# Windowed attention and a hardswish MLP on one core: the output weights loaded before batch 1, and the order of the first 80 microseconds rewritten around that

## The chip, the core and the metric

The kernel runs on 1 core of one Trainium2 chip. The core has a matrix engine (TensorE, PE in the profile), a vector engine (VectorE, DVE), a scalar engine (ScalarE, ACT), GpSimd (POOL) and SyncE (SP), and 16 DMA engines that all queues share. Each engine works through its own list of instructions in order, so an instruction that waits holds up everything listed behind it. The metric is the device time of one execution in microseconds (us), and shorter is better.

## The reference

Attention with a causal window of 64 over 8 batches of 576 tokens, 8 heads of 64; its output, 4608 tokens of 512 values, goes through two matrix products with a hardswish between them.

```python
batch, n_heads, seq, head_dim = (8, 8, 576, 64)
n_tokens, d_model, d_ff = (4608, 512, 2048)
# attention
scores = scale * np.matmul(q, k.transpose(0, 1, 3, 2))
rel = pos[:, None] - pos[None, :]
mask = (rel >= 0) & (rel < window)            # window = 64
scores = np.where(mask, scores, -1000000000.0)
attn = np.exp(scores - max); attn = attn / (sum + 1e-09)
attn_out = np.matmul(attn, v)
# MLP, x = attn_out as (4608, 512)
h = x @ w_in
g = h * np.clip(h + 3.0, 0.0, 6.0) / 6.0
out = g @ w_out
```

The inputs are float32 in DRAM; the loads issued by POOL turn them into bfloat16 on the way into SBUF, and the output is float32.

## The kernel before

**Two kinds of work.** The attention is done two heads at a time: a step `t` is one pair of heads of one batch, four steps (`NG` = 4) to a batch, 32 in all. The MLP is done in blocks of 512 tokens (`TB`), nine in all. A batch has 576 tokens, so block 0 needs only batch 0, and block 1 needs the end of batch 0 and most of batch 1.

**The units of the MLP.** A *first unit* (`unit` in `first_units`, line 472) is four matmuls that make one tile `hT` of 128x512; then ACT makes `t` from it (line 480) and DVE makes one of the 16 columns of `gT` (line 481). Only when DVE is done is the PSUM buffer of `hT` free again. A *second unit* (`unit` in `second_units`, line 500) is four matmuls that add four of those columns, times `wout`, into a tile `acc`; four second units make 128 tokens, which ACT copies to `osb` (line 506) and SP stores (line 508). A block has 16 first units and 16 second units, the second ones as four times four. In this text f8 is the first unit of column 8 of a block, and s0 to s15 are its second units.

**The step of attention**, from batch 1 on: `turn` transposes q and k with matmuls into two PSUM tiles `tk` and `tq` (line 272), `turned` copies them to `KT` (DVE) and `QZ` (ACT) (line 279), `s_first` and `s_rest` make the scores (lines 292, 306), `weights` takes the exponent on ACT (lines 315, 318) and multiplies by a 0/1 band into `P` and `Pz` (lines 323, 326), on POOL or, where the caller says so, on DVE; `pv` multiplies by the values (line 393), `pv_out` divides on DVE (lines 402 to 412), and `x_` moves the result to `xT` by a DMA transpose on SP (line 426), or `x_turned` by matmuls and a copy on ACT (lines 441 to 447). `turn_two` is `turn` and both copies; `front` is the scores and the weights.

**The values** are kept twice, as they come (`Un`) and shifted by 64 tokens (`Us`). `load_v` loads `Un` and the last part of `Us` from DRAM; `shift` then makes the rest of `Us` from `Un` with two SBUF-to-SBUF DMAs on SP (lines 154, 155).

**PSUM.** `ps_t` has three buffers (scores, `hT`, the transposed output), `ps_h` two (`tk` and `tq`, `hT` at some places), `ps_o` one (the result of `pv`), `ps_acc` one (`acc`, and in the first block every second `hT`).

**The order** is written out by hand at the end of the kernel. MLP units wait in a queue, `moe`; `weave(n)` takes n of them. `queue_block(kb)` puts in the 16 first units of block kb, and between them the 16 second units of the block before, which were kept in `left`. Batch 0 has its own early path. Then come the steps of batch 1, with the first units of block 0 between them one at a time, then some units of block 1, and from `group(7, 2)` on a regular loop: `group(t, n)` does `pv(t)`, `turn(t + 2)`, the scores and weights of t + 1, and n units. `late[0]` chooses the PSUM pools.

**The loads.** POOL issues them in program order: q, k and v of batch 0, `w_in` in three parts (line 160), q and k of batch 1 for two steps, v of batch 1, the rest of q and k of batch 1, then `w_out` in two halves (line 166). Each of these DMAs waits until the one eight before it has landed.

The code that the change touches, with the line numbers that the profile uses:

Of the kernel before, what the change touches and what calls it, by code (L numbers as in the profile page):

```python
# [24 lines left out]
P = 128  # L25
D = 64
W = 64
# [9 lines left out]
def kernel(  # L37
# [9 lines left out]
    nc = tc.nc  # L47
# [66 lines left out]
    def load_qk(b, n=NG, first=0):  # L114
        t = staged[b] if first else stage.tile([P, H, RL * D], BF16, name="qk9", tag="qk")
        hs = slice(2 * first, 2 * (first + n))
        for z, src in enumerate((k, q)):
            nc.gpsimd.dma_start(
                out=t[halves[z], hs], in_=src[b, hs].rearrange("h (p r) d -> p h (r d)", r=RL)
            )  # L120
        return t
# [5 lines left out]
                out=Vn[0][:n, m, :, 0:D], in_=v[0, :, m * P : m * P + n, :].rearrange("h s d -> s h d"),  # L127
            )

    def load_v(b):  # L130
        for m in range(3):
            to = Un[b % 2][:, m] if m < 2 else Us[b % 2][3 * P // 4 : P, 1]
            n = 2 * to.shape[0]
            nc.gpsimd.dma_start(  # L134
                out=to[:, :, VO : VO + P],
                in_=v[b, :, 2 * P * m : 2 * P * m + n, :].rearrange("h (p r) d -> p h (r d)", r=2),
            )

    def pads(b, memset):
        for t in (Un[b % 2], Us[b % 2]):  # L140
            memset(t[:, :, :, 0:VO], 1.0)
            memset(t[:, :, :, VO + P : VW], 1.0)
# [345 lines left out]
    def second_units(kb):  # L488
        gT = gTs.pop(kb)
        units = []  # L490
        for ts in range(TB // P):
            state = {}

            def unit(i, ts=ts, state=state):
                if i == 0:
                    pool = ps_t if late[0] == 2 and ts % 2 else ps_acc
                    state["acc"] = pool.tile([P, DM], F32, name="acc", tag="bk")
                acc = state["acc"]
                for fc in range(4 * i, 4 * i + 4):
# [14 lines left out]

    left = []

    def queue_block(kb):

        f, n = first_units(kb), len(left)
        for i, unit in enumerate(f):  # L520
            moe.extend(left[i * n // NFC : (i + 1) * n // NFC])
            moe.append(unit)
        left[:] = second_units(kb)

    def queue_last(kb):

        queue_block(kb)
        queue_block(kb + 1)
        moe.extend(left)
        left.clear()  # L530

    def begin(kb, pools, between):

# [7 lines left out]
    def weave(n):  # L541
        for _ in range(min(n, len(moe))):
            moe.popleft()()
# [108 lines left out]
    for i in range(3):  # L652
        load_w_in(i)
    late_windows()
    staged[1] = load_qk(1, 2)
    load_v(1)
    shift(1)
    load_qk(1, 2, 2)
    for i in range(2):
        load_w_out(i)  # L660
    nc.vector.memset(recs[:], 1.0)
    zero_rows(1)
    nc.vector.memset(Pl[0][:], 1.0)
# [32 lines left out]
    x_early(1)  # L696
    pv_early(3)
    x_early(2)
    queue_block(0)
    begin(0, (ps_acc, ps_t, ps_t), lambda: x_early(3))  # L700
    def group(t, n):

# [21 lines left out]
    def turn_two(t):  # L724
        turn(t)
        turned(t, 0)
        turned(t, 1)

    def front(t, host, muls=(nc.gpsimd,) * 3):
        s = s_first(t, host)  # L730
        weights(t, s, s_rest(t), muls)

    both = (nc.gpsimd, nc.vector, nc.vector)
    n = NG
    weave(4)
    turn_two(n)
    weave(1)
    turn_two(n + 1)
    front(n, n + 1)
    weave(1)  # L740
    front(n + 1, n + 1, both)
    weave(1)
    pv(n)
    pv_out(n)
    x_(n)
    weave(1)
    turn_two(n + 2)
    pv(n + 1)
    pv_out(n + 1)
    x_(n + 1)  # L750
    weave(1)
    turn_two(n + 3)
    front(n + 2, n + 3, both)
    weave(1)
    front(n + 3, n + 3, both)
    weave(1)
    pads(2, nc.gpsimd.memset)
    staged[2] = load_qk(2)
    load_v(2)
    pv(n + 2)  # L760
    pv_out(n + 2)
    weave(1)
# [1 line left out]
    pv_out(n + 3)  # L764
    x_turned(n + 2)
    weave(len(moe))
    late[0] = 1
    queue_block(1)
    weave(1)
    x_turned(n + 3)  # L770
    shift(2)
    weave(9)
    turn_two(2 * NG)
    weave(2)
    group(2 * NG - 1, 2)
    staged[3] = load_qk(3)
    pads(3, nc.gpsimd.memset)
    load_v(3)
    for t in range(2 * NG, T):
# [48 lines left out]
```

## Time and profile before

| what | value |
|---|---|
| time, median of 3 runs | 336.35 us (334.4 to 337.25) |
| time of the profiled execution | 338.35 us |
| its span, first to last instruction | 336.6 us |
| mean granted TensorE clock | 0.974 of full speed |
| PE busy | 308.8 us (92%) |
| ACT, DVE, POOL busy | 188.8, 175.9, 120.4 us |
| moved by DMA | 36.03 MB, mean 107 GB/s |
| one `t` (ACT, line 480), one `gT` (DVE, line 481) | 687 ns, 687 ns |
| one `Pz` on POOL (line 326) | 1145 ns median |
| one `KT` copy (DVE), one `QZ` copy (ACT) | 740 ns, 633 ns |

In the profile, "busy" is the time in which an engine executes; the slices and windows tell where in the span it does. The chain of waits is followed back from the last instruction and tells what released each step. The granted clock is the share of full speed at which PE ran. The times of the runs and the profile's span differ by what lies around the span: 338.35 - 336.6 = 1.75 us for the profiled execution.

### The profile page before, as it was taken

To read this page: it belongs to the slowest core of one execution; us is meant where nothing else is said; L and a number is where in the kernel's file an instruction comes from. 1 tells how busy PE (TensorE), PEld (TensorE's weight loads), DVE (VectorE), ACT (ScalarE), POOL (GpSimd) and SP (SyncE) were. 2 spreads that over 40 slices of the span, in tenths; PEclk is the share of its full clock that TensorE was granted. 3 is DMA by queue.
4 is the path that set the end of the run, shared out by engine and by line. 5 is a ranking of instruction groups with operands and counts; after the bars stand their busy time and mean duration, and the time that the engine had idled before them with its cause. 6 is when DMAs were issued, how large, how long until landed. Compare 5 with 4: busy or idle time off the path is not lost.

```text
span 336.6 us, 11066 instructions
## 1 busy us (share of the span) xinstructions
PE 308.8 (92%) x4770; PEld 157.8 (47%) x4812; DVE 175.9 (52%) x376; ACT 188.8 (56%) x347; POOL 120.4 (36%) x154
## 2 busy tenths in 40 slices
PE   6987367988999999999999999999999999999992
PEld 2843243444455555555555555555544444444440
DVE  7676367355565555555555555555545534444300
ACT  2768435555776666666666666666664444454320
POOL 8942507048645633563356345433330000000000
PEclk9799878999999999999999999999999999999997
DMA  7999992939937932993299429941111110001011
GB/s 92 165 209 190 233 134 34 184 96 162 207 75 127 184 112 57 147 165 112 58 164 148 116 59 187 127 114 53 51 51 51 50 46 31 31 34 62 32 65 68
DMA packets 57032, 36.03 MB, mean 107 GB/s; under 512 B 39184, under 2 KB 50960, under 8 KB 56976
## 3 DMA queue, kind: packets, MB, share of 16 engines
q0 software_dynamic: 33904, 18.35, 42.4%
q1 hardware_dynamic: 23072, 16.89, 20.8%
q8 instruction: 39, 0.64, 0.8%
q14 instruction: 17, 0.14, 0.1%
HBM read 36.70 MB, written 9.44 MB: 137 GB/s over the span
## 4 chain that ended last, share of the span: by engine, by line
PE 78%; DMA 7%; POOL 7%; DVE 2%; issue 2%; ACT 2%; SPq 0%; POOLq 0%; ACTq 0%
PE acc L500 36%; PE hT L472 33%; DMA V<-in_v_dram 5%; PE o L393 4%; PE s L306 2%; DMA V<-V 2%; PE tk L272 1%; POOL qk L107 1%; POOL V L126 1%; POOL Pz L326 1%; ACT t L480 1%; PE tq L272 1%; DVE gT L481 1%; POOL V L134 1%; POOL win L160 1%
## 5 line engine op out<-in xcount | busy, mean ns | idle before, releaser
L481 DVE SCALAR_TENSOR_TENSOR gT<-t,hT 128x512 bf16<-128x512 bf16 x143 | 98.0, 687 | 126.7 <-ACT t L480 126.7
L480 ACT ACTIVATE t<-hT,half_const 128x512 bf16<-128x512 f32 x143 | 97.8, 687 | 97.4 <-PE hT L472 95.3
L472 PE MATMUL hT<-xT,win 128*128 128x512 bf16 x561 | 147.3, 382 | 2.3 <-ACT xT L373 1.0
L500 PE MATMUL acc<-wout,gT 128*128 128x512 bf16 x546 | 143.2, 379 | 2.0 <-issue 0.6
L472 PEld LDWEIGHTS <-win 128*128 128x128 bf16 x576 | 55.8, 99 | 67.6 <-issue 3.0
L500 PEld LDWEIGHTS <-gT 128*128 128x128 bf16 x576 | 54.2, 98 | 63.2 <-issue 0.6
L326 POOL TENSOR_TENSOR Pz<-e,band 128x512 bf16<-128x512 bf16 x53 | 60.2, 1154 | 13.6 <-ACT e L318 13.6
L323 POOL TENSOR_TENSOR P<-e,first 64x256 bf16<-64x256 bf16 x25 | 16.6, 664 | 106.5 <-ACT e L315 106.5
L506 ACT COPY osb<-acc 128x512 f32<-128x512 f32 x36 | 21.1, 587 | 16.7 <-PE acc L500 16.7
L318 ACT ACTIVATE e<-s 128x512 bf16<-128x512 f32 x56 | 30.0, 588 | 0.7 <-PE s L306 0.7
L393 PE MATMUL o<-V,Pz 64*64 64x65 bf16 x1120 | 17.6, 198 | 8.7 <-DMA V<-V 4.0
L393 PEld LDWEIGHTS <-Pz 64*64 64x64 bf16 x1120 | 14.0, 111 | 20.7 <-issue 15.6
L279 DVE COPY KT<-tk 128x576 bf16<-128x576 bf16 x28 | 20.7, 740 | 0.0
L412 DVE TENSOR_TENSOR opl<-o,recs 128x256 bf16<-128x256 f32 x56 | 20.6, 405 | 0.0
L279 ACT COPY QZ<-tq 128x576 bf16<-128x576 bf16 x28 | 17.7, 633 | 0.4 <-PE tq L272 0.4
L134 POOL DMA_DIRECT2D V<-in_v_dram x21 | 16.9, 819 | 0.0
L306 PE MATMUL s<-QZ,KT 64*64 64x64 bf16 x896 | 14.4, 198 | 0.6 <-DVE gT L481 0.6
L272 PE MATMUL tq<-ident,qk 64*64 64x64 bf16 x504 | 14.2, 197 | 0.4 <-DMA qk<-in_q_dram 0.3
L272 PE MATMUL tk<-ident,qk 64*64 64x64 bf16 x504 | 14.6, 197 | 0.0
L315 ACT ACTIVATE e<-tk 64x128 bf16<-64x128 f32 x28 | 7.5, 270 | 12.3 <-PE tq L292 12.3
L272 PEld LDWEIGHTS <-qk 64*64 64x64 bf16 x1008 | 12.1, 107 | 3.6 <-issue 3.3
L306 PEld LDWEIGHTS <-KT 64*64 64x64 bf16 x896 | 11.3, 110 | 0.7 <-issue 0.7
(92 smaller groups left out, 177.1 us busy)
## 6 DMA issues: line engine op xcount, KB each, us to landing
out_dram<-osb SPq DMA_DIRECT2D x36, 256.0 KB, 2.3
V<-in_v_dram POOLq DMA_DIRECT2D x14, 256.0 KB, 5.6
qk<-in_k_dram POOLq DMA_DIRECT2D x6, 576.0 KB, 6.0
qk<-in_q_dram POOLq DMA_DIRECT2D x6, 576.0 KB, 9.6
V<-V SPq DMA_DIRECT2D x7, 432.0 KB, 4.4
wout<-in_moe_w_out_dram POOLq DMA_DIRECT2D x2, 1024.0 KB, 18.0
win<-in_moe_w_in_dram POOLq DMA_DIRECT2D x2, 512.0 KB, 8.6
win<-in_moe_w_in_dram POOLq DMA_DIRECT2D x1, 1024.0 KB, 14.4
```

Of the source, the lines that this page charges most:

```text
L272: nc.tensor.transpose(out=hosts[t][z][halves[h], r * W : (r + 1) * W], in_=staged[b][halves[z], 2 * g + h, r * D : (r + 1) * D], identity= ...
L279: (nc.scalar.copy if z else nc.vector.tensor_copy)(out=(QZ[t % 4][:, 0] if z else KT[t % 4][:, W:]).rearrange("q (p r) -> q p r", r=RL), i ...
L306: nc.tensor.matmul(ss[h][halves[i], c, m, r], lhsT=keys(t, h, W * (w - 1), r), rhs=QZ[t % 4][halves[h], 0, w * W : (w + 1) * W], start=Tru ...
L318: nc.scalar.activation(out=e[:].rearrange("p c m r w -> p (c m r w)"), in_=ss[h][:].rearrange("p c m r w -> p (c m r w)"), func=EXP, scale ...
L326: muls[h].tensor_tensor(out=Pw[t % 4][:, h].rearrange("p c m r w -> p (c m) (r w)"), in0=e[:].rearrange("p c m r w -> p (c m) (r w)"), in1 ...
L393: nc.tensor.matmul(o[halves[c], i, c0 : c0 + D + 1], lhsT=p, rhs=vt[:, 2 * g + h, v0 : v0 + D + 1], start=(r == 0), stop=(r == 1), skip_gr ...
L412: nc.vector.tensor_tensor(out=opg[:, :, i], in0=ov[:, i, 2:6, 1 : D + 1].rearrange("p (m h) d -> p m h d", h=2), in1=rec[:, i, 2:6].rearra ...
L472: nc.tensor.matmul(hT, lhsT=win16[:, g, fc * P : (fc + 1) * P], rhs=xT[:, g, t0 : t0 + TB], start=(g == 0), stop=(g == NG - 1),)
L480: nc.scalar.activation(out=t1[:], in_=hT, func=RELU, bias=half_const[:], scale=1.0 / 6.0)
L481: nc.vector.scalar_tensor_tensor(out=gT[:, fc, :], in0=t1[:], scalar=1.0, in1=hT, op0=MIN, op1=MULT)
L500: nc.tensor.matmul(acc[:], lhsT=gT[:, fc, ts * P : (ts + 1) * P], rhs=wout16[:, fc, :], start=(fc == 0), stop=(fc == NFC - 1),)
L506: nc.scalar.copy(out=osb[:], in_=acc[:])
```

## The change

Six edits, all in the same region of the program:

1. Both halves of `w_out` are loaded right after `w_in`, ahead of q, k and v of batch 1.
2. `load_v` of batch 1 loads the shifted values whole from DRAM (four DMAs of 256 KB in place of two and one of 64 KB), and `shift(1)` goes.
3. Block 0's second units are queued behind its first units (`kept` = 0). Its 13 remaining first units and two second units run ahead of `turn_two(4)`; the other 14 second units stand between the steps of batch 1. All of batch 1's `P` and `Pz` are made on DVE (`own`).
4. The loads of batch 2 are issued ahead of batch 1's attention; those of q and k of batch 3 ahead of `turn_two(8)`.
5. Block 1 begins with `begin`, three first units with their fourth matmul held back until `x_turned(7)` is done. From then on `queue_block` puts the first 8 second units of a block into the block's own batch, behind its 16 first units, and keeps 8 for between the first units of the next block.
6. The `acc` of the second 128 tokens of each block is in `ps_t` (in the last blocks also that of the fourth, as before).

```diff
-    def load_v(b):
-        for m in range(3):
-            to = Un[b % 2][:, m] if m < 2 else Us[b % 2][3 * P // 4 : P, 1]
-            n = 2 * to.shape[0]
+    def load_v(b, whole=False):
+        for m, to, n in (
+            (0, Un[b % 2][:, 0], 2 * P), (2 * P, Un[b % 2][:, 1], 2 * P),
+            *(((W, Us[b % 2][:, 0], 2 * P), (W + 2 * P, Us[b % 2][:, 1], 2 * P)) if whole
+              else ((4 * P, Us[b % 2][3 * P // 4 : P, 1], W),)),
+        ):
...
-                    pool = ps_t if late[0] == 2 and ts % 2 else ps_acc
+                    pool = ps_t if ts == 1 or late[0] == 2 and ts == 3 else ps_acc
...
-    def queue_block(kb):
+    def queue_block(kb, kept=2 * NG):
...
         left[:] = second_units(kb)
+        n = len(left) - kept
+        moe.extend(left[:n])
+        del left[:n]
 
     def queue_last(kb):
-        queue_block(kb)
-        queue_block(kb + 1)
-        moe.extend(left)
-        left.clear()
+        queue_block(kb, NFC)
+        queue_block(kb + 1, 0)
...
     late_windows()
-    staged[1] = load_qk(1, 2)
-    load_v(1)
-    shift(1)
-    load_qk(1, 2, 2)
     for i in range(2):
         load_w_out(i)
+    staged[1] = load_qk(1, 2)
+    load_v(1, True)
+    load_qk(1, 2, 2)
...
-    queue_block(0)
+    queue_block(0, 0)
     begin(0, (ps_acc, ps_t, ps_t), lambda: x_early(3))
...
-    both = (nc.gpsimd, nc.vector, nc.vector)
+    pads(2, nc.gpsimd.memset)
+    staged[2] = load_qk(2)
+    load_v(2)
+    own = (nc.vector,) * 3
     n = NG
-    weave(4)
+    weave(NFC - 3)
+    late[0] = 1
+    weave(2)
     turn_two(n)
     weave(1)
     turn_two(n + 1)
-    front(n, n + 1)
-    weave(1)
-    front(n + 1, n + 1, both)
-    weave(1)
+    front(n, n + 1, own)
+    weave(3)
+    front(n + 1, n + 1, own)
+    weave(3)
     pv(n)
     pv_out(n)
-    x_(n)
+    turn_two(n + 2)
     weave(1)
-    turn_two(n + 2)
     pv(n + 1)
     pv_out(n + 1)
+    x_(n)
+    turn_two(n + 3)
+    weave(1)
+    front(n + 2, n + 3, own)
     x_(n + 1)
     weave(1)
-    turn_two(n + 3)
-    front(n + 2, n + 3, both)
-    weave(1)
-    front(n + 3, n + 3, both)
-    weave(1)
-    pads(2, nc.gpsimd.memset)
-    staged[2] = load_qk(2)
-    load_v(2)
+    front(n + 3, n + 3, own)
+    weave(2)
     pv(n + 2)
     pv_out(n + 2)
     weave(1)
...
     x_turned(n + 2)
     weave(len(moe))
-    late[0] = 1
+    shift(2)
     queue_block(1)
+    begin(1, (ps_acc, ps_t, ps_t), lambda: x_turned(n + 3))
+    staged[3] = load_qk(3)
     weave(1)
-    x_turned(n + 3)
-    shift(2)
-    weave(9)
     turn_two(2 * NG)
-    weave(2)
+    weave(1)
     group(2 * NG - 1, 2)
-    staged[3] = load_qk(3)
     pads(3, nc.gpsimd.memset)
     load_v(3)
```

More of the change, by code (lines that the diff above doesn't have):

```diff
@@ L128, in load_early_v @@
             )
-    def load_v(b):
-        for m in range(3):
-            to = Un[b % 2][:, m] if m < 2 else Us[b % 2][3 * P // 4 : P, 1]
-            n = 2 * to.shape[0]
+    def load_v(b, whole=False):
[4 more added lines that the diff above has]
+        ):
             nc.gpsimd.dma_start(
                 out=to[:, :, VO : VO + P],
-                in_=v[b, :, 2 * P * m : 2 * P * m + n, :].rearrange("h (p r) d -> p h (r d)", r=2),
+                in_=v[b, :, m : m + n, :].rearrange("h (p r) d -> p h (r d)", r=2),
             )
```

## The prediction

> **What bounds the kernel now.** I read the slices of the span first.
>
> ```profile
> PE   6987367988999999999999999999999999999992
> ...
> PEclk9799878999999999999999999999999999999997
> DMA  7999992939937932993299429941111110001011
> ```
>
> A slice is 8.4 us. From the twelfth on PE is at 9 and its clock full: windows of one steady group give 7.95 of 8.00 us busy. That work is the same after the change, so only time that PE loses earlier can be won. The hole lies in slices 4 to 7, and DMA is at 9 up to the sixth. So next, windows of 5 us there (time, PE, PEld, DVE, ACT, POOL, granted clock, DMA share, GB/s):
>
> ```profile
> 30.00:35.00 5.00, 3.13 (x114) 1.73 (x114) 3.76 (x6) 3.25 (x7) 0.18 (x1) 1.00 1.52 192
> 35.00:40.00 5.00, 2.38 (x45) 1.04 (x47) 2.54 (x4) 3.59 (x10) 4.38 (x4) 0.94 1.21 241
> 40.00:45.00 5.00, 3.13 (x92) 1.80 (x95) 1.35 (x5) 0.09 (x1) 0.00 (x0) 0.50 1.22 217
> 45.00:50.00 5.00, 2.81 (x128) 1.88 (x121) 3.88 (x9) 2.36 (x5) 0.00 (x0) 0.84 1.18 98
> 50.00:55.00 5.00, 4.61 (x118) 2.38 (x111) 2.88 (x5) 4.04 (x10) 2.31 (x3) 0.69 0.34 17
> 55.00:60.00 5.00, 3.02 (x62) 1.51 (x61) 4.09 (x13) 2.01 (x3) 4.29 (x9) 1.00 0.65 91
> ```
>
> PE is busy 19.1 of 30 us, part of it at half clock. The waits of 20 to 92 us name the causes (us in all, times, longest):
>
> ```profile
> PE o L393 <- DMA V<-V: 4.0, 1, 4.0
> ...
> PE tk L292 <- DVE KT L279: 3.5, 2, 2.1
> ...
> PE o L393 <- POOL Pz L326: 2.6, 4, 0.9
> PE o L393 <- DVE opl L412: 1.9, 1, 1.9
> ```
>
> They are the shifted values, the copies before a `front`, POOL's bands, and the single buffer of `pv`. Behind these waits stands one first unit at a time: block 0's 16 are all the filler there is, since `w_out` comes last.
>
> **What was lost.** In steady stretches a unit starts every 0.863 us (line 472 at 300.03, line 500 at 300.89). From `turn(4)` at 30.40 to the end of the scores of step 9 at 76.13 (the mark below) are 45.7 us. PE does 9 + 7 first units and 7 second units there (23 x 0.863 = 19.9 us) and the attention: six `turn` at 0.5, six scores at 0.55, five `pv` at 0.55, two transposed outputs at 0.4, together 9.9 to 10. So 15.9 us are lost: the waits above, some 3.2 at half clock (half of PE's 3.8 us in 42 to 46, and 1.3 around 50 to 53), the rest small gaps.
>
> **The change, walked along PE.** Up to f7 at 30.3 nothing differs.
>
> *The other first units.* f6, f8, f10, f12 and f14 now follow each other in the one buffer of `ps_acc`, with only one unit between them. How long a buffer is held is in the timeline (start, us):
>
> ```profile
> 300.03 1.03 PE L472 MATMUL hT<-xT,win 128*128 128x512 bf16 x4
> ...
> 301.10 0.69 ACT L480 ACTIVATE t<-hT,half_const 128x512 bf16<-128x512 f32 x1 [1.04 <-PE hT L472]
> ...
> 301.82 0.69 DVE L481 SCALAR_TENSOR_TENSOR gT<-t,hT 128x512 bf16<-128x512 bf16 x1 [1.04 <-ACT t L480]
> ```
>
> From 300.03 to 302.51 are 2.48 us, so two units take 2.53 in place of 1.73. f6 starts at 29.44, hence f8 at 31.95, f14 at 39.5, s0 (the same buffer) at 42.0: 3.9 us lost, a new wait that the diff doesn't show.
>
> *The loads.* The stream runs at 200 GB/s from 20 us on (windows of 2 us give 175 to 217). `w_in` has landed at 27.5: its last part was issued at 13.1 and took 14.4. `w_out` is 2.1 MB, 10.5 us more at 0.2 MB/us, so 38 to 38.7; the first q and k (0.59 MB; 27.5 to 30.9 before) at 41 to 42; the whole values (1.05 MB) at 47 to 48.2; the rest of q and k at 50.2 to 52. They are wanted: `w_out` at 42.0 (its second half at 44.2, for s2), q and k at 43.7, values at 53, the rest at 53.4. All just in time, the first with some 2 us to spare. Leaving out `V<-V` takes 0.5 MB from the stream and the 6.8 us from 34.73 to 41.56.
>
> *Batch 1, from 42.0.* s0, s1 to 43.7; `turn(4)`; s2; `turn(5)` at 45.1; its copies until 46.5 hold the scores (wait 1.0; 1.36 before); s3 to s5; scores of 5 at 49.8; s6 to s8; `pv(4)` at 53.0, values there, bands long done: DVE's Pz took 0.41 once and 0.99 beside POOL's own; POOL now only issues loads, so I take 0.41 (0.99 would put up to 1.2 us on a `front`, partly covered). `turn(6)`, s9; `pv(5)` waits 0.35 for `pv_out(4)` (1.43 us on DVE); `turn(7)` 0.2; scores of 6 wait 0.9 for a KT copy queued behind `pv_out(5)`; s10 to s13; `pv(6)` at 62; `pv(7)` waits 0.85 for `pv_out(6)`; s15 ends at 65.9. `begin` of block 1: the xT copies cost 0.8. Then ACT and DVE work off four first units at once (4 x 0.69): f4 waits 0.6 for a buffer, `turn(9)` 1.3 for the KT copy behind four gT. `pv(8)` waits 1.5 for POOL's Pz, as before. SP issues `shift(2)` behind the last store, near 69.5, landed by 75; `pv(8)` wants it at 78. Waits: 7.5 us.
>
> *Sum.* From 30.3 to the mark: 9 + 7 first and 16 second units (27.6), attention 10.0, lost 3.9 + 7.5: 49.0, so the mark falls at 79.3, not 76.1, with 9 units more done (7.8): **4.6 us ahead.**
>
> *After the mark.* POOL's two loads of q and k for batch 3 (0.74 + 0.70) leave the queue ahead of step 9's bands, for which `pv(9)` waits until 82: -1.0. In batch 2 the first units are bunched and share `ps_t` with the scores: two waits of about 0.5 in steps 8 and 9: +1.0. In the loop two firsts now follow each other. Until both scores' buffers are read (141.72 in the step whose scores end at 140.4) the third buffer and the next freed one are just enough; ACT has 7.0 and DVE 6.6 us in the fullest step of 8.2: nothing; at worst 0.5 a batch, 2.5 in five. The tail is 72 units, not 80, at one pace: nothing.
>
> **Forecast:** 4.5 us less: the profiled execution 338.35 to 333.9, its span 336.6 to 332.1; against the median 336.35, which lies 2.0 below the profiled time, **331.9**.
>
> **Rivals.**
>
> *Late loads* (ends on the other side). `w_out` took 16.2 and 19.9 us from issue to landing. If that is its own time and not its place in the queue, q and k land at 27.5 + 19.9 + 3.4 = 50.8, `turn(4)` waits 7.1 us, and with the rest of q and k 0.9 later still the sum is 340. It decides from a landing of 48.2 on (43.7 + 4.5). Against it: in 36 to 46, mostly `w_out`, the stream moved 200 GB/s. A smaller form: the values come in pieces of 128 numbers, and while such a load ran (64 to 66) the DMA share was 1.81 against 1.20 at 60 to 62, with 184 GB/s against 205. If a piece cost double, the extra 0.46 MB would take 4.6 rather than 2.3 us, and q and k for `turn(6)`, wanted at 53.4, would land at 54: 0.6 to 1 us, 333. The Trainium skill ("DMA: Bandwidth & Descriptors", Specifications) wants 512 bytes for full rate and has smaller pieces read, changed and written back; by that rule the double price holds, and the 184 GB/s speak against it.
>
> *Clock.* Half clock came only after 4 us of idling; with PE busy 1.43 of 2 us (24 to 26) it stayed 1.00. But between 31 and 42 PE pauses 0.8 us in each 2.5, for five rounds. If the clock fell, a pair would take 3.45, up to 4.6 us in all: 336.5. The Trainium skill ("TensorE: Matmul & The Clock Gate", A second HAM failure mode: psum-queue depth-cycling) describes this pattern: short idling between groups that cycle through PSUM makes the clock swing between half and full. By that rule this rival holds; so far the trace disagrees.
>
> *Bunching.* The 0.5 a batch comes, and the four-at-once pile costs another 1.5: 335.9.
>
> *More.* `ps_acc` comes free earlier or copies overlap better, half of the 11.4 us of waits goes: 326 to 328.
>
> Chances: forecast (329 to 333.4) 0.47; late loads 0.18, half of it small; clock 0.12; bunching 0.12; more 0.11. A measurement of this kernel tells about 1% (3.4 us) from nothing. Faster by over 1% is the forecast but for a twentieth, and *more*: 0.53. Slower by over 1%, the late loads in full and mishaps on top of the clock: 0.13. The rest 0.34. The range leaves out the far end of *more* (0.08) and the late loads in full (0.12): 328.5 to 337.3.
>
> **What would show it.** In the profile after: no `V<-V` wait before `pv(4)`; DVE gT releasing line 472 four times for 0.8 us in 31 to 42; `turn(4)` near 43.7 with no wait, or short, on q and k; clock 1.00 in 40 to 60; the mark near 79; PE full from 90 on. A wait of over 5 us on q, k or `wout`, a clock of 0.5 in 31 to 45, or pauses in PE beyond 100 us would prove the forecast wrong.

## The result, and the profile after

| what | before | after |
|---|---|---|
| median of 18 runs each | 336.3 us (334.4 to 338.76) | 334.4 us (333.66 to 335.12) |
| time of the profiled execution, its span | 338.35, 336.6 us | 334.31, 332.6 us |
| mean granted TensorE clock | 0.974 | 0.989 |
| PE busy | 308.8 us (92%) | 309.0 us (93%) |

The ratio is 0.9941, with a 95% interval from 0.9921 to 0.9962: the change wins 1.9 us, 0.6%. Forecast were 4.5 us; the time itself lies inside the range that the prediction gave. Profile against profile the two executions differ by 4.0 us, so the first thing to see is that the two comparisons do not agree.

The slices of the changed kernel's span (8.3 us each, tenths of busy time, granted clock, DMA):

```profile
PE   5888688777999999999999999999999999999992
...
PEclk9999999799999999999999999999999999999997
DMA  6999999940943974498549646954111200001011
```

The hole of before, where PE was at 3 and 6 and the clock at 7 to 8, is filled: PE is at 6 or more in all slices from the second to the last but one. The clock still dips once, in the eighth slice, where no dip was forecast. The windows show it closer (time, PE, PEld, DVE, ACT, POOL, clock, DMA share, GB/s):

```profile
30.00:35.00 5.00, 3.73 (x17) 1.55 (x16) 3.30 (x5) 2.75 (x4) 0.63 (x1) 1.00 1.24 207
35.00:40.00 5.00, 3.73 (x18) 1.55 (x16) 2.75 (x4) 2.75 (x4) 1.94 (x6) 1.00 1.46 195
40.00:45.00 5.00, 4.37 (x85) 1.91 (x85) 2.13 (x3) 2.01 (x3) 3.03 (x4) 1.00 1.70 188
45.00:50.00 5.00, 4.13 (x114) 2.23 (x102) 1.92 (x5) 3.02 (x9) 0.00 (x0) 1.00 1.22 210
50.00:55.00 5.00, 4.75 (x149) 2.48 (x147) 3.02 (x9) 2.12 (x4) 0.00 (x0) 1.00 1.38 217
55.00:60.00 5.00, 2.56 (x85) 1.42 (x76) 2.40 (x8) 1.25 (x4) 1.36 (x2) 0.91 1.62 173
60.00:65.00 5.00, 5.00 (x98) 2.36 (x97) 2.17 (x6) 2.79 (x7) 0.00 (x0) 0.75 1.39 179
```

From 30 to 55 PE is busy 20.7 of 25 us at full clock. Then come five microseconds with PE busy for 2.56, and behind them five in which it is busy throughout, but at 0.75 of its speed. The waits from 20 to 92 us (us in all, times, longest) put a name to the first of these:

```profile
PE hT L474 <- DVE gT L483: 2.9, 5, 0.6
PE s L308 <- issue: 1.7, 1, 1.7
PE tk L294 <- DVE KT L281: 1.5, 2, 0.9
PE o L395 <- POOL Pz L328: 1.1, 2, 0.9
```

The wait for `V<-V` (4.0 us before) is gone, that for `KT` is down from 3.5 to 1.5 us, that for POOL's `Pz` from 2.6 to 1.1. The waits for `gT` on the first units are the new wait that the prediction read out of the buffers: four of the five, 0.64 us each, lie between 31 and 40 us, and s0, on the same buffer, waits 0.63 at 41.55 (the fifth, 0.4 us, is at 74.6). "issue" is new and was not forecast: PE stands and waits for nothing that the profile shows. The timeline places it (start, duration, engine, line, operation):

```profile
57.33 0.38 PE L308 MATMUL s<-QZ,KT 64*64 64x64 bf16 x21
59.40 0.33 PE L308 MATMUL s<-QZ,KT 64*64 64x64 bf16 x9 [1.69 <-issue]
59.66 1.89 PE L502 MATMUL acc<-wout,gT 128*128 128x512 bf16 x4
```

In the middle of the scores of step 6, after 23 of the 32 matmuls of line 308, PE stands for 1.69 us. The second unit behind it, s11, then takes 1.89 us for four matmuls in place of some 0.86: half clock.

### The profile page after: what moved, and what is told of

Same layout as the page of the kernel before. It is cut to its first block, busy times and chain, and to the rows that moved or that the text cites. A ratio compares the mean times of both kernels' runs of the same rounds, so it can differ in the third digit from the quotient of the medians.

```text
span 332.6 us, 11108 instructions
## 1 busy us (share of the span) xinstructions
PE 309.0 (93%) x4812; PEld 155.3 (47%) x4812; DVE 177.5 (53%) x382; ACT 186.8 (56%) x347; POOL 114.8 (35%) x149
## 4 chain that ended last, share of the span: by engine, by line
PE 80%; issue 7%; POOL 4%; DVE 4%; ACT 2%; DMA 2%; POOLq 0%; DVEq 0%; ACTq 0%
PE acc L502 36%; PE hT L474 35%; PE o L395 4%; PE s L308 2%; DMA V<-in_v_dram 2%; PE tk L274 2%; POOL qk L107 1%; DVE gT L483 1%; ACT t L482 1%; POOL V L126 1%; PE tq L274 1%; DVE opg L361 1%; POOL Pz L328 1%; DVE KT L281 0%; ACT xT L375 0%
## 5 line engine op out<-in xcount | busy, mean ns | idle before, releaser
L474 PE MATMUL hT<-xT,win 128*128 128x512 bf16 x572 | 137.3, 379 | 5.4 <-DVE gT L483 2.9
L502 PE MATMUL acc<-wout,gT 128*128 128x512 bf16 x576 | 138.9, 381 | 0.6 <-DVE gT L483 0.6
L328 POOL TENSOR_TENSOR Pz<-e,band 128x512 bf16<-128x512 bf16 x48 | 54.2, 1146 | 0.0
L325 POOL TENSOR_TENSOR P<-e,first 64x256 bf16<-64x256 bf16 x24 | 15.9, 663 | 108.0 <-ACT e L317 108.0
L281 DVE COPY KT<-tk 128x576 bf16<-128x576 bf16 x28 | 20.7, 740 | 2.4 <-PE tq L274 2.2
L404 DVE TENSOR_REDUCE sums<-o 128x12 f32<-128x24 f32 x28 | 5.0, 180 | 29.9 <-PE o L395 29.9
L136 POOL DMA_DIRECT2D V<-in_v_dram x22 | 17.9, 821 | 6.4 <-DMA win<-in_moe_w_in_dram 5.3
L395 PEld LDWEIGHTS <-Pz 64*64 64x64 bf16 x1120 | 13.2, 108 | 14.3 <-issue 8.9
L395 PE MATMUL o<-V,Pz 64*64 64x65 bf16 x1120 | 16.6, 195 | 2.0 <-POOL Pz L328 1.1
```

The lines of the kernel that those rows point to most:

```text
L281: (nc.scalar.copy if z else nc.vector.tensor_copy)(out=(QZ[t % 4][:, 0] if z else KT[t % 4][:, W:]).rearrange("q (p r) -> q p r", r=RL), i ...
L328: muls[h].tensor_tensor(out=Pw[t % 4][:, h].rearrange("p c m r w -> p (c m) (r w)"), in0=e[:].rearrange("p c m r w -> p (c m) (r w)"), in1 ...
L395: nc.tensor.matmul(o[halves[c], i, c0 : c0 + D + 1], lhsT=p, rhs=vt[:, 2 * g + h, v0 : v0 + D + 1], start=(r == 0), stop=(r == 1), skip_gr ...
L474: nc.tensor.matmul(hT, lhsT=win16[:, g, fc * P : (fc + 1) * P], rhs=xT[:, g, t0 : t0 + TB], start=(g == 0), stop=(g == NG - 1),)
L502: nc.tensor.matmul(acc[:], lhsT=gT[:, fc, ts * P : (ts + 1) * P], rhs=wout16[:, fc, :], start=(fc == 0), stop=(fc == NFC - 1),)
```

## The experiments

Each kernel was compared with the kernel before on its own chip, whose median was 336.2 to 337.2 us; so ratios are compared, or kernels that shared a chip.

### The kernel before, again

No edit. A second profiled execution tells which part of the first was its own.

> The kernel before, unchanged, timed and profiled again. Theory A: the profiled execution of before (338.35 us) was a long one, 2 us above the median of 336.3, and what was long in it lies in the hole between 30 and 76 us (waits on loads, half clock). Then this profile, if its own time is near 336.3, loses about 14 us there in place of 15.9, with the scores of step 9 ending near 74 in place of 76.1, and the runs of before scatter with their granted clock. Rival B: the hole costs 15.9 us in every execution and the changed kernel loses about 2 us somewhere that the forecast did not have; then this profile has the scores of step 9 at 76 whatever its time, and spans do not follow the clock.

Measured: 337.18 us (334.67 to 338.7), ratio 1.0008 [0.9972, 1.0045]. In its profiled execution (337.5 us, span 335.8) the scores of step 9, the prediction's mark, end at 74.62 us; in the first (338.35, span 336.6) at 76.13. What follows the mark is nearly the same, 261.2 and 260.5 us. So these two executions differ ahead of the mark. The start of the same row of first units splits that stretch, in the first execution and in this one:

```profile
26.21 2.53 PE L472 MATMUL hT<-xT,win 128*128 128x512 bf16 x11 [0.73 <-ACT xT L373]
25.36 2.53 PE L472 MATMUL hT<-xT,win 128*128 128x512 bf16 x11 [0.73 <-ACT xT L373]
```

Of the 1.5 us, 0.85 lie ahead of these first units, and so ahead of the hole (the clock from 5 to 15 us was 0.83 in the first and 1.00 in this one), and 0.66 in the hole (49.92 and 49.26 us from there to the mark). Both executions are longer than the median; one near the median was not profiled. The kernel before scatters over 4.4 us, the changed kernel over 1.5.

### PE kept busy in the hole

```diff
+    warm(ps_acc, 12)
     pv(n)
```

The kernel before, with 12 matmuls that nobody reads ahead of `pv(4)`, where PE waits for `V<-V`. They are work that the reference does not ask for.

> The kernel before, with 12 dummy matmuls of 128x512 (2.6 us at full clock) put ahead of pv(4), where PE waits about 4 us for the shifted values; they compute nothing that is used. If PE's granted clock, falling in that hole, makes the scatter of before (time against clock over 29 runs: 1.6 us per 0.01 of clock): the median falls from 336.5 to 334.5 to 335.3, the clock is at 0.99 or over in nearly all runs and the slowest runs, at 338 to 339, are gone. If the scatter comes from when the values land, with the clock only following: 336.5 with the same scatter. If the dummies delay pv(4): over 337.

Measured: 335.75 us (334.4 to 337.29), ratio 0.9984 [0.9959, 1.0009]. The windows of its profiled execution, which was its fastest:

```profile
40.00:45.00 5.00, 3.87 (x171) 2.27 (x169) 3.78 (x12) 2.44 (x4) 0.00 (x0) 1.00 1.24 207
45.00:50.00 5.00, 2.38 (x78) 1.45 (x79) 3.48 (x7) 3.27 (x10) 1.49 (x2) 1.00 1.07 88
```

The clock was 0.50 and 0.84 there before and is 1.00 now, and the mark is at 72.30. Yet the median moves by 0.6 us only, within its uncertainty, and the scatter stays (3 us). The filling did not do as much in every execution, though: the six that took 336.1 us or more had mean clocks of 0.981 to 0.990, the profiled one 0.999. So what the half clock is worth in the hole, and how much of the scatter comes from it, stays open.

### The order without the loads

```diff
-    for i in range(2):
-        load_w_out(i)
     staged[1] = load_qk(1, 2)
     load_v(1, True)
     load_qk(1, 2, 2)
+    for i in range(2):
+        load_w_out(i)
```

The changed kernel with `w_out` behind batch 1 again, as before.

> The changed kernel with one part undone: w_out is loaded behind q, k and v of batch 1 again, all else as changed. If w_out's place carries the change: the stream of 0.2 MB/us has w_out's halves landed near 45.5 and 51 in place of 32 and 37, s0 waits some 4 us and s2 some 3 more, sum 5.5 to 7 us above the changed kernel, 340 to 341, and slower than before. If the loads are hidden anyway: 334.4, no difference.

Measured: 341.01 us (338.56 to 342.15), ratio 1.0163 [1.0121, 1.0204]. From its waits, 20 to 92 us:

```profile
PE acc L502 <- DMA wout<-in_moe_w_out_dram: 3.6, 2, 2.2
```

The new order needs `w_out` early. Edit 1 is worth some 2.2% inside it and cannot be judged alone. In the changed kernel the loads were on time: PE waits for neither q and k nor `wout` nor V between 30 and 57 us.

### The first units of block 0 in two buffers

```diff
-pool = (ps_h, ps_h, ps_o)[fc - 3] if fc < 6 else ps_t if fc % 2 else ps_acc
+pool = (ps_h, ps_h, ps_o)[fc - 3] if fc < 6 else ps_t if fc % 2 else ps_h
```

The changed kernel with f6 to f14 in the two buffers of `ps_h`, not the one of `ps_acc`.

> The changed kernel, but f6, f8, f10, f12 and f14 go into the two buffers of ps_h in place of the one of ps_acc. The forecast put 3.9 us on that single buffer. If nothing stands right behind it: s0 at 38 in place of 41.6 and the time 331. If the loads stand behind it (q and k land near 41, values near 48, the rest of q and k near 51): turn(4) waits for q and k at 40.6 in place of 43.4, or pv(4) and turn(6) wait for theirs; gain 1 to 2.8, 331.6 to 333.4. If PE's clock or something else decides: under 0.5.

Measured: 331.6 us (331.07 to 332.47), ratio 0.988 [0.9842, 0.9917]. The windows:

```profile
30.00:35.00 5.00, 5.00 (x24) 2.29 (x24) 3.87 (x6) 3.69 (x6) 0.63 (x1) 1.00 1.24 207
35.00:40.00 5.00, 5.00 (x25) 2.28 (x24) 3.94 (x7) 3.60 (x6) 1.94 (x6) 1.00 1.42 196
```

PE is busy 10.00 of 10 us, where it was at 7.46. s0 starts at 38.59 in place of 41.55 and the mark is at 78.55 in place of 81.65. So the one buffer cost 3.0 us up to s0, or 3.6 counted from the first units, which start at 26.29 in this execution and at 25.70 in the other (forecast 3.9); `w_out` had landed, since no wait on `wout` appears. The stall among the scores of step 6 is there too, 0.95 us.

### The second products in their own batch

```diff
         if g == 0 and b > 2:
-            queue_block(b - 1)
+            queue_block(b - 1, NFC)
```

The changed kernel, but from block 2 on all 16 second units of a block are kept for the next batch, as before the change.

> The changed kernel with the second half of edit 5 undone from block 2 on: all 16 second units of a block stay between the first units of the next block, as before (block 1 still gives 8 to batch 2, so batch 3 has 24 units in place of 32 and the tail 8 more). If the bunching in the loop costs nothing, as the forecast has it: 334.4, within 0.4. If it costs 0.5 us a batch: 332 to 332.5. If units in the own batch are worth something in the loop: over 335.

Measured: 339.64 us (337.94 to 340.17), ratio 1.01 [1.0057, 1.0143]. Not a clean test of the bunched first units: keeping more leaves batch 3 with 24 units in place of 32. The windows there:

```profile
120.00:125.00 5.00, 3.48 (x129) 1.93 (x128) 2.41 (x6) 2.52 (x6) 0.44 (x2) 1.00 0.59 129
125.00:130.00 5.00, 4.69 (x23) 2.10 (x23) 3.14 (x7) 3.29 (x7) 2.60 (x3) 1.00 0.21 36
```

PE loses 2.7 us of 50 between 100 and 150, where the changed kernel loses nothing (50.00 busy). The part that can be read: bunched first units cost nothing in the loop (49.96 and 50.00 of 50 us between 150 and 250 in the changed kernel), so the rival *bunching* falls.

### The values: whole, and shifted

Two kernels, the second edit taken out of the changed kernel and put alone into the kernel before.

```diff
 # changed kernel, values shifted
-    load_v(1, True)
+    load_v(1)
+    shift(1)
 # kernel before, values whole
-    load_v(1)
-    shift(1)
+    load_v(1, True)
```

> The changed kernel with that part undone: values of batch 1 loaded once and shifted by SP. In the changed order pv(4) comes at 52, the values land near 44 and 6 to 7 us of shifting end at 51: hidden, 334.4, within 0.5. If the shift ends later than 52: up to 3 slower, 335.5 to 337.

> The kernel before with another part alone: the shifted values of batch 1 are loaded whole from DRAM, and shift(1) goes. pv(4) waits 3 to 4 us for them before; whole they land near 37, when pv(4) comes up. If that wait and the half clock behind it carry the hole: 332.5 to 333.5 and less scatter. If the work behind it then waits for q and k of steps 6 and 7, or for the copies and bands on DVE and POOL, in its place: 335 to 336.4.

Measured: the changed kernel with shifted values 333.35 us (332.44 to 335.76), ratio 0.9876 [0.9848, 0.9904], rather faster than with whole ones. Its `pv(4)`, at 54.02, waits for nothing: the shift has time in the new order. And PE has no stall among the scores of step 6 (58.93 to 59.4). This profiled execution does not show where the gain lies: at 335.76 us it is the slowest of the six, its first units start at 27.36, and from there to the mark it takes 55.8 us, as long as the changed kernel (55.95), since `pv(7)` waits 1.98 us for DVE where it waited 0.57. The kernel before with whole values 336.22 us (334.76 to 337.95), ratio 0.9972 [0.9945, 0.9998]. Its waits from 20 to 92 us:

```profile
PE o L395 <- POOL Pz L328: 3.3, 5, 0.9
PE tk L294 <- DVE KT L281: 2.7, 2, 1.8
PE o L395 <- DVE opl L414: 2.0, 2, 1.3
PE o L395 <- issue: 1.6, 1, 1.6
```

The 4.0 us for `V<-V` are gone, and the bands on POOL, the buffer of `pv` and an "issue" of 1.6 us stand in their place. In the old order the longest wait hid the next ones.

### The bands of batch 1

```diff
-    own = (nc.vector,) * 3
+    own = (nc.gpsimd, nc.vector, nc.vector)
...
-    front(n, n + 1, own)
+    front(n, n + 1)
```

> The changed kernel with the bands of batch 1 made where they were before (step 4 on POOL, then one head of two on POOL). A Pz costs POOL 1.15 and DVE 0.41 to 0.46 us in the profiles, 1.0 on DVE when both work. If bands are off the path (pv comes 3 us after its scores): 334.4, within 0.5. If pv(6) or pv_out, behind the bands on DVE, pay: 335 to 336.

Measured: 335.62 us (334.83 to 337.02), ratio 0.9943 [0.9911, 0.9975]. No difference from the changed kernel: DVE or POOL, the bands of batch 1 are made in time. The stall is there, 1.99 us.

### The loads of q and k of batch 3

The prediction gave this move 1.0 us. It was made alone in the kernel before, on two chips:

```diff
+    staged[3] = load_qk(3)
     turn_two(2 * NG)
     weave(2)
     group(2 * NG - 1, 2)
-    staged[3] = load_qk(3)
```

> The kernel before with one part of the change alone: the loads of q and k of batch 3 are issued ahead of turn_two(8). In the profiles PE gains 1.4 us in step 8 (pv(9) waits for bands that POOL made late) and 0.5 behind it. If that is the gain of the change that reaches the end: 334.6 to 335.2 against 336.4. If pv(9) then waits for something else: 336.4, within 0.4.

> The kernel before with only the loads of q and k of batch 3 moved ahead of turn(8), once more on another chip, since its first six times lay at two levels (333.15 to 334.09 and 336.8). If this move alone carries the whole gain: 0.988 to 0.994, as the changed kernel. Rival: the first result was a draw of good executions; then 0.996 to 1.

Measured: 333.97 us (four of six at 333.15 to 334.09, two at 336.8), ratio 0.9902 [0.9865, 0.994]; and 334.87 us (333.51 to 337.64), ratio 0.9966 [0.9934, 0.9998]. The sign is the same, the size is not: in a kernel that scatters as this one does, a third to one per cent. `pv(9)` waits for no band in either. But `pv(8)` has a new wait, 0.7 and 1.2 us for `V<-V`, and PE stands 0.7 and 1.0 us on "issue" ahead of a `turn` near 93 us. Both profiled executions are long ones of their kernel (336.84 and 337.64 us), so they do not show where the shorter ones win.

Then it was taken out of the changed kernel, beside the changed kernel on one chip:

```diff
-    staged[3] = load_qk(3)
     weave(1)
     turn_two(2 * NG)
     weave(1)
     group(2 * NG - 1, 2)
+    staged[3] = load_qk(3)
```

> The changed kernel once more, beside the next three on one chip, so that their differences can be read without a change of chip. Expected 0.990 to 0.998 of the kernel before, and again PE standing 1 to 2 us with no wait that the profile shows among the scores of step 6, some 57 to 58 us into the span.

> The changed kernel with the loads of q and k of batch 3 issued behind group(7) again, as before the change; nothing else. If the 1.7 to 1.9 us that the changed kernel won after the end of step 9's scores come from this move, as the same move alone in the kernel before suggests (0.990), pv(9) waits 1 to 1.5 us for its bands on POOL again and the time goes up by 1.3 to 2 us, to the kernel before's own: 0.998 to 1.001. Rival: the wait was already covered by the five units ahead of pv(9), and the time stays at 0.994.

Measured: the changed kernel 334.42 us (334.03 to 334.69), ratio 0.9916 [0.9883, 0.9949]; without the move 337.94 us (337.06 to 339.33), ratio 1.0053 [1.0024, 1.0082]. So the other five edits together make the kernel no faster, rather slower by half a per cent, and in this order the move carries the whole gain: 3.5 us between the medians, 2.6 between the spans (335.5 and 332.9). Up to the mark the two profiles agree (81.85 and 81.93). Behind it, in the waits from 76 to 100 us, the kernel without the move has

```profile
PE o L395 <- POOL Pz L328: 2.5, 4, 0.9
PE tq L274 <- issue: 1.6, 1, 1.6
```

where the changed kernel has 1.1 us for `Pz` and no "issue". The 1.4 us are the wait of `pv(9)` for bands that stand on POOL behind two issues of 0.73 and 0.68 us, as the prediction said. The other 1.6 is again a stall without a wait, this time ahead of a `turn` at 94.83.

### The stall: which loads run then

First q and k of batch 3 were issued later in the changed kernel, behind `pads(3)`, near 68 us and not 56.

```diff
     begin(1, (ps_acc, ps_t, ps_t), lambda: x_turned(n + 3))
+    pads(3, nc.gpsimd.memset)
     staged[3] = load_qk(3)
...
     group(2 * NG - 1, 2)
-    pads(3, nc.gpsimd.memset)
```

> The changed kernel, but the memsets of batch 3's value buffers stand ahead of the loads of its q and k, so that these are issued when pv(7) is done (near 67) and not at 56. The changed kernel's PE stands 1.7 us in the scores of step 6 with nothing that the profile shows as releaser, in the microsecond in which one 16 KB packet of instructions is fetched, with a DMA share of 1.6. If the fetch is slow because of the loads beside it: the stall is under 0.6, the half clock behind it is gone, 332 to 333. If the fetch takes as long whatever moves beside it: 334.4, within 0.4.

Measured: 334.76 us (333.18 to 335.84), ratio 0.9941 [0.9919, 0.9963]; the stall is there, 1.70 us. These loads do not cause it. What runs at 56 to 58 us is the end of batch 2's loads. So batch 2's values (0.6 MB) were put behind a band of step 6:

```diff
     staged[2] = load_qk(2)
-    load_v(2)
...
-    front(n + 2, n + 3, own)
+    front(n + 2, n + 3, (nc.gpsimd, nc.vector, nc.vector))
+    load_v(2)
```

> The changed kernel with batch 2's values (0.6 MB) issued by POOL behind a band of step 6, near 60 us, and not ahead of batch 1's attention. If the stall of 1.7 us among the scores of step 6 (57 to 59 us) comes from the load stream that still runs then, nothing but the end of q and k is left in the queue at 57 and the stall goes, with the half clock behind it: 0.984 to 0.989 of the kernel before; a stall may then come where the values land, 61 to 65 us. Rival: the stall belongs to that place in the program, whatever is loaded; then it stays within 0.5 us of the changed kernel's and the time too, 0.994.

Measured, on the chip of the two kernels above: 331.25 us (331.1 to 331.96), ratio 0.9823 [0.9773, 0.9874], 3.2 us less than the changed kernel beside it. There is no "issue" among its waits, and its windows are

```profile
55.00:60.00 5.00, 3.97 (x164) 2.46 (x165) 3.38 (x10) 2.47 (x7) 0.83 (x1) 1.00 0.31 66
60.00:65.00 5.00, 4.32 (x114) 2.33 (x114) 3.23 (x11) 1.34 (x5) 4.05 (x6) 1.00 0.91 122
```

The stall and the half clock behind it are gone together, and the mark falls at 79.42. So the stall depends on what the DMA engines do at that time; its place in the program alone does not make it. (The edit also moves one band of step 6 to POOL. That is not what helps: the kernel with all three edits, further down, has the same band on POOL, and the stall.) The queues tell more. In the changed kernel, from 57 to 58 us (packets, MB, and the time of the packets as a share of 16 engines' time, which passes 100% where packets overlap; q0 are POOL's loads, q1 SP's DMAs, q8 instructions; then an issue and its time to landing):

```profile
q1 hardware_dynamic: 251, 0.06, 234.3%
q0 software_dynamic: 247, 0.06, 62.0%
q8 instruction: 1, 0.02, 5.9%
...
xT<-opg SPq DMA_TRANSPOSE x1, 7.8
```

and with batch 2's values later, from 56 to 57:

```profile
q1 hardware_dynamic: 499, 0.13, 63.2%
...
xT<-opl SPq DMA_TRANSPOSE x1, 2.6
xT<-opg SPq DMA_TRANSPOSE x1, 2.3
```

SP's DMAs at that time are the transposes of `x_(4)` (line 428). Alone they move 499 packets in a microsecond with 63% and land in 2.3 to 2.6 us. Into the end of the load stream they move 251 packets with 234%, and one takes 7.8 us. A packet then takes 0.15 us in place of 0.02 (an estimate: the share times 16 us, over the packets). In that same microsecond one packet of instructions is fetched, and PE stands. The second stall, of the kernel with q and k of batch 3 late, has the same picture: an instruction packet at 92 to 93 us, transposes issued at 89.92 and 91.19 into batch 3's loads, and from 93 to 94 us

```profile
q1 hardware_dynamic: 515, 0.13, 214.7%
q0 software_dynamic: 135, 0.03, 37.4%
```

with PE standing from 93.3 to 94.8.

The transposes are not needed for it, though. In the kernel with two buffers, whose stall of 0.95 us runs from 54.77 to 55.72, POOL's loads fill the engines by themselves, from 54 to 55 us:

```profile
q0 software_dynamic: 515, 0.16, 146.9%
q1 hardware_dynamic: 23, 0.03, 11.1%
```

Common to the stalls of 0.88 us and more is an instruction packet, in the microsecond in which the stall begins or up to two and a half ahead of it, and DMA engines with over 100% of packet time behind that packet. One stall, of 0.88 us with three units moved, has neither: its packet is over three microseconds ahead, and the engines are at 66%.

### Several edits together

Three kernels were built on the two buffers: with `turn(8)` moved into the beginning of block 1 and `pads(3)` earlier; with that and three second units moved; and the first of these with shifted values.

```diff
-    begin(1, (ps_acc, ps_t, ps_t), lambda: x_turned(n + 3))
+    begin(1, (ps_acc, ps_t, ps_t), lambda: (x_turned(n + 3), turn_two(2 * NG)))
+    pads(3, nc.gpsimd.memset)
     staged[3] = load_qk(3)
-    weave(1)
-    turn_two(2 * NG)
-    weave(1)
+    weave(2)
     group(2 * NG - 1, 2)
-    pads(3, nc.gpsimd.memset)
```

> Two buffers for f6 to f14 (331.6 alone), the loads of q and k of batch 3 later, and turn_two(8) put between the three first units of block 1 and their fourth matmuls. The walk has turn(9) wait 0.7 to 1.3 behind the KT copy of step 8, which DVE does after four gT, and 0.7 for the xT copy; with turn_two(8) ahead both are covered: 1.5 to 2 us less than the two buffers alone, 329.5 to 330, and 0.5 to 1.5 less again if the later loads help, 328.5. If those waits only move on to pv(8), which waits for POOL: 331 or more.

> As the run with turn_two(8) in begin, with three second units moved: s11 ahead of the scores of step 6 (which wait 0.7 for a KT copy), one unit less ahead of pv(6), s14 and s15 between pv(6) and pv(7) (which waits 0.6 to 1.2 for pv_out(6)). If each unit of 0.86 us fills the wait that it is moved to: 1 to 1.5 us less than that run. If the waits follow the units: no difference, or up to 0.7 more since the xT copy behind x_turned(6) then has nothing beside it.

> Three things together that each helped alone: the even first units f6 to f14 in the two buffers of ps_h (-2.5 us against the changed kernel), turn(8) inside the beginning of block 1 (-0.5 to -1), and batch 1's values shifted on SP as before the change, not loaded whole (-0.65% or 2.2 us, mostly the stall among the scores of step 6). If the three add up: 0.975 of the kernel before, some 328 us. Rival: with the second units from 38.6 on, pv(4) comes 3 us earlier, near 50, and the two shifts on SP are not done by then; then pv(4) waits on V<-V for 1 to 3 us and the time is that of the kernel with whole values, 0.981.

Measured: 330.47 us (330.04 to 331.23), ratio 0.981 [0.9771, 0.9849]; 330.4 us, ratio 0.9806 [0.9765, 0.9846]; 331.83 us (331.7 to 332.64), ratio 0.9848 [0.9795, 0.9901]. Moving the units does nothing. Shifted values do not add to the two buffers: with everything 3 us earlier `pv(4)` waits 2.0 us for `V<-V`. In this last one the transposes also jam, from 56 to 57 us,

```profile
q1 hardware_dynamic: 323, 0.08, 304.4%
q0 software_dynamic: 276, 0.07, 72.3%
```

but the instruction packet had come at 55 to 56, ahead of the jam, PE reached the place 2 us later, and stood for 0.23 us only. So a jam does not make a stall by itself. If PE waits for instructions, it must be short of them at that moment; no run shows that directly.

At last the two buffers, `turn(8)` and the later values of batch 2 in one kernel:

> The changed kernel with the three edits that each took a measured loss away: even first units in ps_h (2.5 us), turn(8) inside the beginning of block 1 (0.5 to 1 us), batch 2's values issued behind a band of step 6 (3.2 us). If the losses are separate: 331.25 - 3.5 = 328, ratio 0.972 to 0.976, no stall among step 6's scores and clock 1.00 in 30 to 90 us. Rival: with everything 3 us earlier, the loads of batch 1 (on time by some 2 us only) or batch 2's values are late; then a wait on q, k or V appears and the time stays at 330 to 331, 0.981.

Measured: 329.88 us (329.19 to 331.67), ratio 0.9814 [0.9779, 0.9849]. The gains do not add. PE waits 0.9 us for q of batch 1, which it now reaches nearly 3 us earlier, and the stall is back, 1.5 us, at the same place of the program. From 54 to 55 us (packets, MB, share):

```profile
q1 hardware_dynamic: 308, 0.10, 260.0%
q0 software_dynamic: 21, 0.02, 11.6%
```

The transposes now come 3 us earlier, at 51.7, while q and k of batch 2 and a store of 256 KB still run; batch 2's values are not the point by themselves. This kernel, the first two of the three above and the one with the later values alone lie at 0.981 to 0.982 of the kernel before, with intervals that overlap: 5 to 6 us faster than before and some 3 to 4 faster than the change.

## Why the prediction was wrong

The sign, the waits and most of the walk were right; the size was not. Two steps failed. What the first one cost is shown by runs; of the second only an estimate can be given.

**The first failed step: "Waits: 7.5 us" from 42.0 to the mark.** The walk was right up to the scores of step 6 (its 58.1 is worked out from the walk):

| event (us) | forecast | measured |
|---|---|---|
| s0 starts | 42.0 | 41.55 |
| `turn(4)` | 43.7 | 43.37 |
| scores of 5 | 49.8 | 49.22 |
| `pv(4)` | 53.0 | 52.36 |
| scores of 6 | 58.1 | 57.27 |
| mark | 79.3 | 81.65 |
| mark, batch 2's values later | | 79.42 |

Then came the stall (1.7) and the half clock behind it (1.0 on s11 alone, 1.89 for 0.86). The sum held no term for either: it put at nothing what the load stream does to an engine that waits for none of the loads. The mark is 2.35 us late, or 2.9 counted from the first units, which start at 25.70 in this execution and at 26.21 in the one that was walked. With batch 2's values out of the way (first units at 26.28) the mark is where the walk had put it, within 0.1 us. That the load stream at that time decides over the stall is shown: with batch 2's values later it is gone. That PE waits for its instructions there is argued, from the packet of instructions ahead of each stall but one and the full DMA engines behind it; many packets also pass under a full stream without one.

**The second failed step: from the profile to the median.** "the profiled execution 338.35 to 333.9 ... against the median 336.35, which lies 2.0 below the profiled time, 331.9" takes the same 4.5 us off both. What made that one execution 2.0 us longer than the median cannot be won from the median a second time, as far as it lay in the hole that the change fills. Some 0.5 to 0.85 us of it lay ahead of the first units, and not in the hole (26.21 against 25.70 in the changed kernel and 25.36 in the second profile). The rest is an estimate: after the mark both profiled executions of before need 260.5 to 261.2 us; the median execution has a span near 336.35 - 1.75 = 334.6, so its mark is near 73.4 to 74.1. The changed kernel's is at 81.65, less 9 units x 0.863 = 7.8, so 73.9. By this estimate next to nothing was won ahead of the mark against the median, and the 15.9 us of lost time were some 1 to 2 too many. The row that should have warned was the scatter of the times itself, 334.4 to 337.25, with a profiled execution above all three.

**Mis-sized: "After the mark", forecast 0.** Before, the rest took 260.5 us with 9 units more, so 252.7 for equal work; after, 332.6 - 81.65 = 250.95: 1.8 us won. In the profile before, two waits from 76 to 100 us make up that much, and neither is there after (the 1.1 us for `Pz` there are `pv(8)`'s, ahead of the mark):

```profile
PE o L393 <- POOL Pz L326: 1.3, 2, 0.8
PE s L306 <- DVE gT L481: 0.6, 1, 0.6
```

The first is the wait of `pv(9)`, forecast as 1.0. In the new order the move of q and k was worth more, 2.6 us, since there it took away a stall (1.6) that the kernel before does not have, beside the wait of `pv(9)` (1.4). "Bunching: +1.0" was not seen: five units run ahead of `pv(9)`, and from the mark to 100 us no wait of this kind is left.

**Luck.** Against the profiled execution the forecast came out within half a microsecond: 338.35 became 334.31, the span 336.6 became 332.6 where 332.1 was forecast. But a mark 2.35 us too late and 1.8 us won behind it, where nothing was forecast, cancel there (-4.6 + 2.35 - 1.8 = -4.05; the terms are read off the same marks, so they must close). The 331.25 us with batch 2's values later, beside the forecast 331.9, are such a meeting too: the 1.8 us behind the mark stand against the 2.0 that were taken off twice.

**The other steps.** *One buffer of `ps_acc`*: right, the new wait is there on four first units and on s0, 0.63 to 0.64 us each (forecast 0.8), and two buffers give 3.0 to 3.6 us of the 3.9. *Loads*: right, all in time and 1 to 3 us ahead of the forecast (`w_out` landed at 36.6, the last of the values near 45.5). The rival *late loads* falls in both forms. The page "DMA: Bandwidth & Descriptors" of the Trainium skill (Specifications) wants 512 bytes for full rate; the double price was the prediction's reading of it. From 40 to 46 us, while the whole values landed, the stream kept 182, 185 and 208 GB/s, so the price was about a tenth at most and not double. The whole values may have had a price all the same, through the stall: the run with shifted values has none. *Clock*: the reading "Half clock came only after 4 us of idling" did not fit the prediction's own rows, where 50 to 55 us has 0.69 behind a wait of 2.1 us that ended at 49.6. In 30 to 40 us, with PE pausing in each round, it stayed at 1.00, so the rule of the Trainium skill ("TensorE: Matmul & The Clock Gate", A second HAM failure mode) on groups that cycle through PSUM did not hold at 3.73 of 5 us busy. Half clock came behind the 1.7 us stall instead. *Taking away `V<-V`*: its 4.0 us were counted as won with the rest of the hole; alone, in the old order, they are worth 0.3%, and in the new order the shift was in time anyway.

## What to carry to other kernels

One profiled execution that is slower than the median is not the kernel: find where it is slower (a profile of an execution near the median would show it) before taking a hole in it off the median. A wait that lands on "issue" in the middle of a row of equal matmuls is worth a look at the DMA queues of that microsecond, and loads are worth moving out of it even when nobody waits for them. When several edits come together, take each out of the new kernel and put each alone into the old one: here one moved load carried the gain in the new order, and one buffer cost more (3.0 us in the profiles) than the whole change won (1.9).

## What was not expected of the hardware

- DMA transposes into a running load stream are slow: the two transposes of `x_(4)` land in 2.6 and 2.3 us with batch 2's values later, and in 5.6 and 7.8 us in the changed kernel, beside the end of batch 2's loads. There 251 packets took 234% of the engines' time, where 499 took 63% alone; over 200% is seen in such a microsecond in several of the kernels (304% at most).
- PE can stand without any wait of its own. It stood 0.95 to 2.0 us among the scores of step 6 in ten of the profiles here, in nine of them after the 23rd of the 32 matmuls, and at other places too (1.64 us ahead of a `pv` in the kernel before with whole values, 1.56 us ahead of a `turn` with q and k of batch 3 late), in the same microsecond as a 16 KB packet of the instruction queue or shortly behind it, with the DMA engines full. The Trainium skill ("Runtime: NRT & Kernel Launch", Instruction fetch mechanics) has each engine fetch its program in blocks of 16 KiB over a DMA queue of its own while it executes, with the cost of a block "mostly hidden". The size agrees with the packets of the trace; hidden it was not, if that is what PE waited for. What stays open: in the kernel with all three edits PE stood until 56.5, though the DMA engines were nearly idle from 55 to 56 (share 0.26), and no run here shows which engine a packet is for.
- Half clock followed a stall of 1.7 us in which PE, from 55 to 60 us, was busy 2.56 of 5 us; without the stall, at 3.97 of 5, the clock stayed at 1.00. That is no rule: in the kernel before with q and k of batch 3 early, waits of 2.1 and 2.5 us left PE busy 2.37 and 2.52 of 5 us from 45 to 55, and the clock stayed at 1.00 there and in the five microseconds behind. What decides is not settled.
- The kernel before scatters over 3.4 to 5.0 us on every chip and the changed one over 0.7 and 1.5, though both do the same work. Part of the scatter lies ahead of the hole (the first units start between 25.3 and 27.4 us in the profiled executions); filling the hole with idle matmuls did not take it away, so its cause is not settled.
